# Issuing some of the weight loads in mid-run, in pieces, in a kernel that mixes sliding-window attention and a SwiGLU block

## The chip, the cores and the metric

The kernel runs on one core of one Trainium2 chip. The metric is the device time of one execution in microseconds (us), median of the runs. The engines are TensorE (PE; its weight loads are listed apart as PEld), VectorE (DVE), ScalarE (ACT), GpSimd (POOL) and SyncE (SP), which issues nearly all DMAs. The times of the profile come from one profiled execution.

## The reference

Shapes: S = 2048 tokens, D = 512, 32 heads of 16, window W = 256, F = 1376, all bf16.

```python
x = A_x
g = sigmoid((x * gate_w).sum(-1, keepdims=True))
# A: attention of 32 heads, causal, each query sees the last 256 keys
qkv = (x @ wqkv).reshape(B, S, 3, H, Dh).transpose(2, 0, 3, 1, 4)
scores = einsum("bhqd,bhkd->bhqk", q, k) * (Dh ** -0.5)
mask = (idx[:, None] - idx[None, :] >= 0) & (idx[:, None] - idx[None, :] < W)
p = softmax(where(mask, scores, -1e9))
a = einsum("bhqk,bhkd->bhqd", p, v).transpose(0, 2, 1, 3).reshape(B, S, D) @ wo
# B: SwiGLU
b = einsum("bsf,fd->bsd", silu(x @ w1) * (x @ w3), w2)
out = g * a + (1 - g) * b
```

## The kernel before

All weights stay in SBUF: w1, w3 (512 x 1376), w2 (1376 x 512), the Q, K, V weights (512 x 1536) and the output weights `wo` (512 x 512). x is held transposed in `xT`, in four quarters of 512 tokens. Its first quarter is loaded plain and turned by TensorE; the other three are turned by DMA transposes (`turn_x`, four DMAs of 512 tokens x 128 columns each). w1, w3 and the Q, K, V weights come in column pieces (`load_w`).

`opening` (L301) issues, in this order on SP: half of the first x rows, K weights, Q weights, first pieces of w1 and w3, V weights (first 256 columns of each of K, Q, V), x quarter 1 (counted from 0), w1 columns 256 to 768 and w3 the same, w1 and w3 columns 768 to 1376, x quarter 2, w2 in two DMAs, x quarter 3, `wo`, and the second 256 columns of K, Q, V. The engines' constants are made beside this.

Everything else is given to a planner (`Plan`). Each step has an engine, a duration, the steps it depends on, a due time and buffers that it takes and frees. `emit` lists the steps greedily: it takes the engine that can start earliest, and on it, of the steps that can start then, the one with the earliest due time. The result is a fixed order of instructions on each engine; on the chip the engines wait for each other by semaphores alone, and the planner's times have no force. When a load is in is told to the planner by the table `landed` (L337).

The attention runs over c = 0 to 3, each of 8 heads (128 columns of Q, K, V). For each c: projections of K and Q (L425) and V (L483) for each quarter, scores in blocks of 128 keys (`main_batch` L544, `edge_batch` L594), exponentials on ACT (L548, L598), masks on POOL (L553, L558, L611), the products with V (`pv`, L684), and a normalization on DVE that ends in the tile `OT` (L718). c = 0 and 1 use the first 256 columns of K, Q, V, c = 2 and 3 the second.

The SwiGLU block runs over four quarters of tokens (`tcb`), each over eleven pieces f of F: gate and up products (L809), Tanh on ACT (L819), two products on DVE (L823, L829) into `hT`. The last piece is only 96 wide. 64 of its rows go through `wA`; the other 32 are computed by tokens (`tail_columns`, L769, with `wB`), end on DVE in `hb` (L783), and are turned into `hX` by four DMA transposes on SP (`tr_b`, L793). `wA` and `wB` are copied out of w1 and w3 on POOL (L747). Then the products with w2 follow (L859) and an eviction scaled by 1 - g. The output projection (L889), the sum (L893) and the stores (L899) come last.

Semaphores make SP wait in its own order: a DMA stands behind all that were listed on SP before it.

## Time and profile before

| | |
|---|---|
| median of 3 runs | 238.67 us (238.44 to 240.37) |
| profiled execution, its time | 242.65 us |
| its span, first to last instruction | 240.9 us |
| PE busy | 229.0 us, 95% of the span |
| DVE, ACT, POOL busy | 185.6, 178.4, 154.5 us |
| PE by line, share of the chain that ended last | L809 28%, L859 16%, L425 11%, L684 9%, L544 8% |
| "issue" in that chain | 4% |
| DMA queue q1 (SP's transfers) | 10.59 MB |
| instruction queues q8 and q14 | 0.48 MB in 29 packets, 0.07 MB in 8 |

How to read it: the page divides the span into 40 equal slices of 6.02 us. A digit gives an engine's busy share of a slice in tenths, "PEclk" the clock that TensorE was granted, in tenths of full speed, "DMA" the mean busy share of the core's 16 DMA engines, and "GB/s" what they moved. The chain of waits goes back from the last instruction to what released each step; "issue" is time in which the engine waited for nothing that the profile shows. In a table of groups or waits, `a <-b` names what ended a wait.

SP's issues, in order of time (start, length and count; the length runs from the first issue of the row to the end of its last, waits included):

```profile
4.97 5.11 SPq L288 DMA_TRANSPOSE xT<-in_A_x_dram  x4
10.12 2.56 SPq L295 DMA_DIRECT2D w_sb<-in_B_w_dram  x4
12.73 7.53 SPq L288 DMA_TRANSPOSE xT<-in_A_x_dram  x4
20.30 0.58 SPq L320 DMA_DIRECT2D w_sb<-in_B_w_dram  x1
20.93 0.68 SPq L322 DMA_DIRECT2D w_sb<-in_B_w_dram  x1
21.66 6.00 SPq L288 DMA_TRANSPOSE xT<-in_A_x_dram  x4
27.70 0.58 SPq L324 DMA_DIRECT2D wo_sb<-in_A_wo_dram  x1
28.33 2.66 SPq L295 DMA_DIRECT2D wqkv_sb<-in_A_wqkv_dram  x3
31.10 174.76 SPq L793 DMA_TRANSPOSE hX<-hb  x16
```

### The profile page before, as it was taken

Reading aid. Unit: us, or ns where it says so; the run is one execution under the profiler, and the core shown is the slowest. Engines: PE = TensorE matmul, PEld = TensorE weight load, DVE = VectorE, ACT = ScalarE, POOL = GpSimd, SP = SyncE. Lnnn points to the kernel's source line nnn. Section 1 sums busy time; section 2 is a strip of 40 time slices with the busy share of each in tenths; the row PEclk is TensorE's granted clock in tenths of the full one; section 3 lists DMA queues with packets and bytes.
Section 4 is the critical chain, followed back from the end, with each engine's and each line's share of the span. In section 5 each row is a group of like instructions: output and inputs, shape, how many; then the busy total and the mean of one; then the engine's idle time right before and its main releaser. Section 6 shows DMA issues by size and latency. Waiting matters only on the chain.

```text
span 240.9 us, 8477 instructions
## 1 busy us (share of the span) xinstructions
PE 229.0 (95%) x3700; PEld 119.0 (49%) x3738; DVE 185.6 (77%) x322; ACT 178.4 (74%) x153; POOL 154.5 (64%) x257
## 2 busy tenths in 40 slices
PE   8999679999999999999999999999999999999994
PEld 8554423645553454545555555545454546354542
DVE  5477927697779895986878797798876978987945
ACT  3589818887679898878689898987789898976000
POOL 7169655498776768476577786774859785856000
PEclk9999958999999999999999999999999999999999
DMA  7999990000000001000000001000000001020322
GB/s 200 200 346 234 208 238 6 3 4 0 3 5 0 3 3 22 3 4 3 3 3 3 4 0 25 3 0 5 4 0 3 3 1 23 6 67 24 100 79 87
DMA packets 20413, 11.59 MB, mean 48 GB/s; under 512 B 9656, under 2 KB 20376, under 8 KB 20376
## 3 DMA queue, kind: packets, MB, share of 16 engines
q1 hardware_dynamic: 19680, 10.59, 18.7%
q8 instruction: 29, 0.48, 0.9%
q10 hardware_dynamic: 696, 0.46, 0.6%
q14 instruction: 8, 0.07, 0.1%
HBM read 6.85 MB, written 2.10 MB: 37 GB/s over the span
## 4 chain that ended last, share of the span: by engine, by line
PE 90%; issue 4%; ACT 2%; DVE 2%; DVEq 0%; ACTq 0%
PE ch L809 28%; PE ch L859 16%; PE ch L425 11%; PE ch L684 9%; PE su L544 8%; PE ch L483 6%; PE ch L889 5%; PE su L594 2%; PE su L299 1%; PE ch L769 1%; ACT Ee L598 1%; ACT tt L819 1%; PE ch L362 1%; DVE hT L829 1%; DVE h L823 1%
## 5 line engine op out<-in xcount | busy, mean ns | idle before, releaser
L548 ACT ACTIVATE Em<-su 128x2048 bf16<-128x2048 f32 x60 | 112.6, 1877 | 19.5 <-PE su L544 16.7
L809 PE MATMUL ch<-xT,w_sb 128*128 128x512 bf16 x301 | 79.3, 388 | 1.9 <-issue 1.0
L553 POOL TENSOR_SCALAR_AFFINE_SELECT Em<-Em 64x512 bf16<-64x512 bf16 x60 | 42.5, 709 | 37.0 <-ACT Em L548 32.4
L611 POOL TENSOR_SCALAR_AFFINE_SELECT Ee<-Ee 64x1024 bf16<-64x1024 bf16 x32 | 37.2, 1162 | 16.1 <-ACT Ee L598 14.9
L809 PEld LDWEIGHTS <-w_sb 128*128 128x128 bf16 x320 | 29.1, 99 | 35.9 <-issue 8.8
L823 DVE SCALAR_TENSOR_TENSOR h<-tt,ch 128x512 bf16<-128x512 bf16 (+1 forms) x44 | 29.7, 678 | 14.4 <-ACT tt L819 13.9
L859 PE MATMUL ch<-w_sb,hT 128*128 128x512 bf16 x152 | 38.3, 380 | 0.9 <-issue 0.8
L558 POOL TENSOR_SCALAR_AFFINE_SELECT Em<-Em 64x512 bf16<-64x512 bf16 x56 | 36.8, 658 | 3.3
L501 POOL COPY vs<-vs 64x256 bf16<-64x256 bf16 (+1 forms) x80 | 31.6, 395 | 9.8 <-DVE vs L496 6.6
L598 ACT ACTIVATE Ee<-su 128x2048 bf16<-128x2048 f32 x16 | 30.0, 1877 | 7.3 <-PE su L594 5.4
L425 PE MATMUL ch<-xT,wqkv_sb 128*128 128x512 bf16 (+1 forms) x128 | 33.6, 371 | 0.6 <-issue 0.3
L829 DVE SCALAR_TENSOR_TENSOR hT<-h,ch 128x512 bf16<-128x512 bf16 x40 | 27.1, 677 | 7.6 <-PE ch L809 5.5
L819 ACT ACTIVATE tt<-ch 128x512 bf16<-128x512 f32 (+1 forms) x44 | 26.0, 594 | 6.4 <-DVE vs L496 3.3
L684 PEld LDWEIGHTS <-vs 128*17 128x17 bf16 x1664 | 20.5, 92 | 6.3 <-issue 5.1
L859 PEld LDWEIGHTS <-hT 128*128 128x128 bf16 x160 | 14.3, 98 | 16.9 <-issue 2.5
L684 PE MATMUL ch<-Em,vs 128*17 128x256 bf16 (+2 forms) x672 | 22.5, 242 | 0.0
L684 PE MATMUL ch<-Ee,vs 128*17 128x64 bf16 x992 | 22.1, 193 | 0.0
L483 PEld LDWEIGHTS <-xT 128*128 128x128 bf16 x256 | 15.7, 98 | 8.1 <-issue 4.8
L425 PEld LDWEIGHTS <-wqkv_sb 128*128 128x128 bf16 x136 | 12.5, 99 | 13.7 <-issue 2.7
L544 PE MATMUL su<-qT,kz 32*128 32x256 bf16 x240 | 17.4, 280 | 0.6
L544 PE MATMUL su<-qT,k 32*128 32x256 bf16 x240 | 16.8, 270 | 0.0
L544 PEld LDWEIGHTS <-kz 32*128 32x128 bf16 x240 | 6.0, 91 | 19.2 <-issue 17.4
(77 smaller groups left out, 252.5 us busy)
## 6 DMA issues: line engine op xcount, KB each, us to landing
out_dram<-ot SPq DMA_DIRECT2D x15, 128.0 KB, 1.7
wqkv_sb<-in_A_wqkv_dram SPq DMA_DIRECT2D x5, 256.0 KB, 5.4
w_sb<-in_B_w_dram SPq DMA_DIRECT2D x1, 1280.0 KB, 7.0
w_sb<-in_B_w_dram SPq DMA_DIRECT2D x2, 608.0 KB, 8.5
w_sb<-in_B_w_dram SPq DMA_DIRECT2D x2, 512.0 KB, 4.5
w_sb<-in_B_w_dram SPq DMA_DIRECT2D x2, 256.0 KB, 4.8
wo_sb<-in_A_wo_dram SPq DMA_DIRECT2D x1, 512.0 KB, 5.4
xs<-in_A_x_dram SPq DMA_DIRECT2D x1, 256.0 KB, 2.9
```

Of the source, the lines that this page charges most:

```text
L425: nc.tensor.matmul(pst[:, t0:t1], lhsT=wqkv_sb[:, dc, col + c * P:col + (c + 1) * P], rhs=xT[:, dc, tq * 512 + t0:tq * 512 + t1], start=(d ...
L501: nc.gpsimd.tensor_copy(out=v_of(to, base, a), in_=v_of(half, 0, a))
L544: nc.tensor.matmul(su[:, s, a * 256:(a + 1) * 256], lhsT=head_keys(r, t, a), rhs=qT[r, q0:q0 + 256], start=True, stop=True)
L548: nc.scalar.activation(out=Em[job.at["Em"]][:], in_=su[:].rearrange("p s (a q) -> p s a q", a=2), func=ACT.Exp, scale=SCALE)
L553: nc.gpsimd.affine_select(out=e, in_=e, pattern=[[0, 8], [1, KB]], compare_op=ALU.is_ge, fill=0.0, base=0, channel_multiplier=-1)
L558: nc.gpsimd.affine_select(out=e, in_=e, pattern=[[0, 8], [-1, KB]], compare_op=ALU.is_ge, fill=0.0, base=-1, channel_multiplier=1)
L598: nc.scalar.activation(out=Ee[ej.at["Ee"]][:].rearrange("p s t k q -> p s (t k q)"), in_=su[:], func=ACT.Exp, scale=SCALE)
L611: nc.gpsimd.affine_select(out=e, in_=e, pattern=[[0, 4], [0, 4], [1, KB]], compare_op=ALU.is_ge, fill=0.0, base=0, channel_multiplier=-1)
L684: nc.tensor.matmul(po[32 * s:32 * s + VW, lo - 512 * w:hi - 512 * w], lhsT=vs[:, i, a * VW:(a + 1) * VW], rhs=mov, start=(n == 0), stop=(n ...
L809: nc.tensor.matmul(ch[job.at["ch"]][:], lhsT=wA[:, dc, :] if joint else w[:, dc, f * P:(f + 1) * P], rhs=xT[:, dc, tcb * 512:(tcb + 1) * 512],
L823: nc.vector.scalar_tensor_tensor(out=h1[job.at["h1"]][ru, :], in0=tt[job.at["tt"]][rg, :], scalar=1.0, in1=ch[job.at["ch"]][rg, :], op0=AL ...
L859: nc.tensor.matmul(bps[:], lhsT=ht[:, mm * P:(mm + 1) * P], rhs=w2_sb[0:fs, f, :], start=(f == 0), stop=(f == NFC - 1))
```

## The change

The loads of w2, of `wo` and of the second half of the Q, K, V weights leave the opening. w2 is loaded in four pieces (four, four and two of its eleven blocks of rows, then the last), each listed on SP behind one of the four `hX` transposes of the first quarter. The second half of Q, K, V and then `wo` become steps of the planner on SP that it may not place before its time 86. In the opening, the last pieces of w1 and w3 are now issued between the DMA transposes of x quarter 2. The planner's dates for x quarters 2 and 3 are altered.

```diff
-    def turn_x(tq):
-        for c in range(NDC):
+    def turn_x(tq, c0=0, c1=NDC):
+        for c in range(c0, c1):
...
+    def load_w2(f0, f1):
+        nc.sync.dma_start(out=w2_sb[:, f0:f1, :], in_=B_w2[f0 * P:f1 * P, :].rearrange("(f p) n -> p f n", p=P))
+    def load_w2_end():
+        nc.sync.dma_start(out=w2_sb[0:FL, NFC - 1, :], in_=B_w2[(NFC - 1) * P:F, :])
+    def load_wo():
+        nc.sync.dma_start(out=wo_sb[:], in_=A_wo.rearrange("(c p) n -> p c n", p=P))
...
-        for f0, f1 in ((2 * P, 6 * P), (6 * P, F)):
-            load_w(w1_sb, B_w1, f0, f1)
-            load_w(w3_sb, B_w3, f0, f1)
-        turn_x(2)
-        nc.sync.dma_start(out=w2_sb[:, 0:NFC - 1, :],
-                          in_=B_w2[0:(NFC - 1) * P, :].rearrange("(f p) n -> p f n", p=P))
-        nc.sync.dma_start(out=w2_sb[0:FL, NFC - 1, :], in_=B_w2[(NFC - 1) * P:F, :])
+        load_w(w1_sb, B_w1, 2 * P, 6 * P)
+        load_w(w3_sb, B_w3, 2 * P, 6 * P)
+        turn_x(2, 0, 1)
+        load_w(w1_sb, B_w1, 6 * P, F)
+        turn_x(2, 1, 2)
+        load_w(w3_sb, B_w3, 6 * P, F)
+        turn_x(2, 2, 4)
         turn_x(3)
-        nc.sync.dma_start(out=wo_sb[:], in_=A_wo.rearrange("(c p) n -> p c n", p=P))
-        for b in (1, 0, 2):
-            load_w(wqkv_sb, A_wqkv, b * D + 2 * P, (b + 1) * D)
...
-    landed = {"x": [3.7, 4.45, 12.2, 21.2, 30.2], "w13": [7.1, 8.0, 15.4, 18.7], "w2": 28.0,
-              "qkv": [5.25, 6.15, 8.8, 36.0], "wo": 32.0, "gw": 5.8}
+    landed = {"x": [3.7, 4.45, 12.2, 22.5, 28.5], "w13": [7.1, 8.0, 15.4, 18.7],
+              "qkv": [5.25, 6.15, 8.8], "late": 86.0, "gw": 5.8}
...
-    w2_in, wo_in = arrive(landed["w2"]), arrive(landed["wo"])
+    prev = arrive(landed["late"])
+    for b in (1, 0, 2):
+        prev = add("SP", 0.6, lambda b=b: load_w(wqkv_sb, A_wqkv, b * D + 2 * P, (b + 1) * D), [prev], landed["late"],
+                   lat=0.0 if b < 2 else 4.0)
+    qkv_in.append(prev)
+    wo_in = add("SP", 0.6, load_wo, [prev], landed["late"], lat=4.0)
...
                 res.append(add("SP", 1.25, tr_b, [a] + wx_done.get(tcb - 2, []), due, lat=1.3))
+                if tcb == 0:
+                    load = load_w2_end if mm == 3 else lambda f0=(0, 4, 8)[mm], f1=(4, 8, 10)[mm]: load_w2(f0, f1)
+                    w2_in.append(add("SP", 0.6, load, [res[-1]], due, lat=4.0))
...
-                           hs[f0:f1] + ([prev] if prev else [w2_in]), due,
+                           hs[f0:f1] + ([prev] if prev else w2_in), due,
```

More of the change, by code (lines that the diff above doesn't have):

```diff
@@ L751 @@
     b_ready = {}
+    w2_in = []
     last_up = []
```

## The prediction

> **What bounds the kernel now.** I read the page's slices first, then the chain of waits, the stretches around the one hole that it shows, and the instruction queues in the DMA rows.

> ```profile
> PE   8999679999999999999999999999999999999994
> ...
> PEclk9999958999999999999999999999999999999999
> DMA  7999990000000001000000001000000001020322
> ```

> TensorE is full (digit 9) in nearly every slice. The exceptions are the ends and slices 5 and 6 (24 to 36 us), and only behind them, in slices 6 and 7, is the clock low. The DMA row is full in the first six slices alone. The chain of waits shows what the low digits are:

> ```profile
> 27.78 0.34 PE ch L483 x4
> 28.12 3.41 issue
> 31.53 0.59 PE ch L483 x4
> 32.12 0.43 PE ch L809
> 32.55 0.22 issue
> 32.77 2.77 PE ch L809 x6
> ...
> 39.88 1.73 PE ch L809 x8
> ```

> TensorE stands for 3.41 us and waits for nothing that the profile names. The V product that follows (L483) is the last quarter of one whose other three had run, so its data were there. Afterwards six products of L809 take 2.77 us (0.46 each); later eight take 1.73 (0.216 each). The stretches give the clock:

> ```profile
> 15.34:26.24 10.90, 10.63 (x136) 4.94 (x140) 8.48 (x18) 10.08 (x11) 10.06 (x20) 1.00 1.22 290
> 26.24:28.12 1.88, 1.88 (x112) 1.53 (x101) 1.87 (x7) 1.08 (x4) 1.28 (x2) 1.00 1.34 172
> 28.12:31.53 3.41, 0.00 (x1) 0.00 (x0) 1.43 (x6) 1.62 (x1) 2.36 (x6) 0.86 1.32 131
> 31.53:37.40 5.87, 5.65 (x23) 2.14 (x24) 2.52 (x7) 1.95 (x3) 1.83 (x3) 0.50 0.83 210
> 37.40:48.00 10.60, 10.55 (x190) 5.44 (x191) 7.50 (x14) 8.52 (x11) 5.92 (x11) 1.00 0.01 2
> ```

> Columns: stretch, length, busy time and count of PE, PEld, DVE, ACT, POOL, then clock, DMA share, GB/s. From 31.53 to 37.40 TensorE is busy at clock 0.50, and from 37.40 on busy and at full clock, 10.55 of 10.60 us.

> What it stood for: queue q8 moved 29 instruction pages, 0.48 MB, so 16 KB each; TensorE has 7,438 recorded instructions, 256 to a page. Up to 15.34 it had started 125 + 130 = 255, and a page moves between 15 and 16 us: when one page is used up, another is asked for. Up to 26.24 it has started 255 + 276 = 531, two pages, but the next page moves only in this window, from 28.9 to 29.0 us:

> ```profile
> q1 hardware_dynamic: 89, 0.02, 96.2%
> q8 instruction: 1, 0.02, 69.1%
> ```

> At 28.12 the count is 531 + 213 = 744, close to three pages of 256 (semaphore instructions are not in it). So I read the hole as a code page that came 2.7 us late behind the kernel's own transfers. The page takes 1.1 us (69.1% of 16 engines in 0.1 us), ends at 30.0, and TensorE goes on 1.5 us later. The burst of 160 small instructions at 25.98 to 27.1 (L684) made it need the page so early. This is inferred, not labelled.

> **What the hole costs.** 3.41 us of standing and half of the 5.87 us at half clock, 2.94: 6.35 us. As TensorE is full behind it, all of that reaches the end. The profiled execution took 242.65 us (span 240.9 and 1.75 around it); without the hole it would be 236.3. The median of the runs, 238.67, is 3.98 below the profiled execution and 2.4 above 236.3. I read that as a shorter hole without the slow clock in most runs; the 240.37 among them fits a longer one. So on the median the hole is worth some 2.4 us, not 6.35, and this decides the forecast.

> **The change, part by part.**

> *Taken out of the opening:* six DMAs of SP (w2 1,280 and 96 KB, output weights 512, three of 256). The two of w2 stood ahead of the last four x transposes: 1.41 MB at the 323 GB/s of 22 to 26 us is 4.4 us of transfer.

> *Order on SP.* After the first x transposes end at 10.08 us: loads at 0.64 each (2.56 for four), transposes at 1.88 (7.53 for four). Two w loads end at 11.4, a transpose at 13.3, w1's end at 13.9, a transpose at 15.8, w3's end at 16.5, two transposes at 20.2, the last four (1.28 to 1.88 each) at 25.3 to 27.7, where before they end at 27.66. Their last landed 5.2 us after its issue before and 2.7 in the first group: 26.7 to 31, against 31.5. I take 28, as w2 no longer lies ahead. Third-quarter x: last issue at 18.3 instead of 18.4, landing 3.4 later as before, 22: no change. Nobody waits for x earlier than before, so that saves nothing by itself.

> *w3's last part* is issued at 15.8 instead of 11.9, 3.9 us later. It landed 8.5 us after issue, at 20.4; a load with less ahead took 4.5 to 5.4. So it lands at 20.4 to 24.3. Its first user is the copy on POOL at 22.88 (L747), behind which the masks of line 553 are queued, and behind those the products of L684. Price: 0 to 1.4 us; I take 0 and keep 1.4 (the slot on SP, not the bytes, sets the time).

> *w2 in pieces behind the hX transposes of the first quarter.* The transposes wait for hb (28.10 + 0.25) and were held by SP's loads to 31.10, so they can go at 28.4. Four at 1.41 (5.64) and four loads at 0.64 end at 36.6; the last hX issue moves from about 35.3 to 34.6; the last piece lands 5 to 8.5 us behind its issue, 41 to 45. The first use is L859 at 49.6: 4 us or more of cover. Cost nothing; without the cover, the 4 us at full.

> *Late loads* (three of 256 KB, one of 512): on SP they stand either right behind these (36.6 to 39.2, landed by 46) or behind the second quarter's hX transposes, which in the trace end at 95.3, then 97.9, landed by 104. The first use of these Q, K, V weights is the product at 109.25, of the output weights at 207.4. Cover 5 us even then. No semaphore wait is added that stands long; the product of the first quarter now waits for four loads instead of one.

> *Planner.* Three dates change (21.2 to 22.5, 30.2 to 28.5, w2's gone), so the order on the engines can change from about 20 us on. The trace can't show it. TensorE is full behind 37.4, so an order is worth little except at the ends: I give it 1 us either way, a third of the 3 us between its last product at 237.7 and the span's end.

> *The code page.* At 26.2 us the last x transposes are still in flight, as before, but with 4.4 us less ahead; there is a lull until hX at 28.4. If the page is asked for at 26.2, takes 1.1 us and the same 1.5 to restart, TensorE goes on at 28.85, 0.7 us late; if the 1.5 was itself the crowd, nothing is lost. With the old delay it loses 3.41 again. I take 0.7: a gap this size leaves the clock alone, as all later gaps do.

> The sum, against the profiled execution: 242.65 - 3.41 + 0.7 - 2.94 = 237.0. Against the median, 2.4 - 0.7 = 1.7 off: 237.0 too.

> [...]

> **Rivals.**

> 1. *The hole goes entirely* (0.32): the request meets the lull. For it: from 37.4 to 48, with DMA at 0.01, a page moves and TensorE loses 0.05 us. 236.3, give or take the 1 us of order.
> 2. *The hole isn't the loads' doing* (0.08): it is something that no load order moves. For it: the chain names no releaser. 238.7.
> 3. *w3's end late on POOL* (0.06): 237.0 + 1.4 = 238.4; it decides once it lands after 22.9.
> 4. *Slower: the hole moves and grows* (0.18). Transfers now run without a break from 2 to about 46 us where before they end near 36; the hX transposes lie among w2's pieces, and 256-byte transpose packets were what lay ahead of the late page. If a page is asked for among them and a burst such as L684's (224 instructions, 1.46 us at 45.99) follows, TensorE stands 3.4 us or more, and the clock falls: 6.35 on top of 236.3 is 242.7. It decides at a wait of about 3.4 us, the one that was followed by 0.50. Against it: the page at 35.2, also amid transfers, stopped nothing, since only 47 instructions ran in 5.87 us.

> **Chances and range.** Forecast 0.36, rivals 0.32, 0.08, 0.06, 0.18. One per cent of 238.67 is 2.39 us, about what a measurement of this kernel tells from no change: 236.28 to 241.06. Faster: half of rival 1, whose centre lies on that bound (0.16), and a third of the forecast through the order (0.12): 0.28. Slower: rival 4 and a mishap of order in rival 3 (0.02): 0.20. The rest, 0.52, is within. The range runs from 235.4 (rival 1 less 0.9 of its order) to 241.3, between the forecast and rival 4, which is mostly left out; the forecast's own range is 236 to 238.

> **What would show it.** A gap of TensorE below 1 us around 28, clock 1.00 in slices 5 to 7, x's last quarter landing before 31, and q8's second page moving before 28. SP's late loads either near 37 or near 95, with nobody waiting for them. I am wrong if the profile shows a long gap at another page, if POOL waits before L747, or if the gap at 28 is there with the page on time.

## The result, and the profile after

| | before | changed |
|---|---|---|
| median of 22 runs each | 240.77 us (238.44 to 243.43) | 238.66 us (237.13 to 241.07) |
| profiled execution, its time | 242.65 us | 237.91 us |
| its span | 240.9 us | 236.2 us |
| PE busy | 229.0 us | 225.6 us |

The ratio of the changed kernel to the one before is 0.9923, 95% interval 0.9896 to 0.995: faster by 0.77%, clear of no change, and inside the 1% of the likeliest case. The ratio leaves out the runs that lie more than 1.5% above the fastest of their kernel, so it is not the quotient of the two medians. The level of the kernel before, 238.67 in its first three runs, turned out to be low: the 22 runs have a median 2.1 us higher.

The planner's dates changed, but the compiled lists of instructions of TensorE, VectorE, ScalarE and GpSimd are the same, row by row, in both kernels. Only SP's list differs. So every difference in time comes from when transfers run.

The slices of the page of the changed kernel:

```profile
PE   8999899999999999899999999999999999999994
...
PEclk9999999999999999999999999999999999999999
DMA  7999262000000005200000000000000001010322
```

The low TensorE digits and the low clock in slices 5 to 7 are gone. A slice is 5.9 us here. The DMA row is low in slice 4 (23.6 to 29.5 us), and new work stands in slices 15 and 16 (88.6 to 100.4 us); in slice 16 TensorE has an 8. The chain of waits of the changed kernel (start, length, what), around 28 us and around 96 us:

```profile
27.37 0.34 PE ch L494 x4
27.71 0.76 issue
28.47 0.39 PE ch L494 x4
28.86 0.22 PE ch L824
29.07 0.05 issue
29.13 1.46 PE ch L824 x6
...
95.95 0.34 PE su L605 x30
96.29 0.75 issue
97.04 0.20 PE su L605 x2
```

L494 is the V product that was L483 before. It is cut at the same place, but the gap is 0.76 us instead of 3.41, and six products behind it take 1.46 us instead of 2.77. At 96.29 there is a new gap, inside a batch of scores (L605), with two products of 32 to go. Before, that batch ran through:

```profile
101.79 0.34 PE su L594 x32
102.13 0.75 PE ch L809 x3
```

The late loads stand just ahead of the new gap. SP's issues in the changed kernel:

```profile
84.51 4.92 SPq L805 DMA_TRANSPOSE hX<-hb  x4
89.47 1.68 SPq L295 DMA_DIRECT2D wqkv_sb<-in_A_wqkv_dram  x3
91.19 0.51 SPq L304 DMA_DIRECT2D wo_sb<-in_A_wo_dram  x1
```

An instruction page begins to move behind them; the DMA rows from 94.5 to 94.7 us (queue and kind: packets, MB, share of 16 engines):

```profile
q1 hardware_dynamic: 77, 0.08, 107.6%
q8 instruction: 1, 0.02, 29.2%
```

So the 4.7 us of span divide as follows (times before and after of the same piece of the chain). A row of eleven L859 products starts at 52.99 before and at 47.15 after: 5.84 us won. Nine L809 products start at 99.68 and at 93.85: still 5.83. The V products of 16 start at 102.89 and at 98.00: 4.89. Here 0.94 us is given back, 0.75 of it in the new gap. At the end 4.7 are left.

### The profile page after: what moved, and what is told of

Same layout as the page of the kernel before. It is cut to its first block, busy times and chain, and to the rows that moved or that the text cites. A ratio compares the mean times of both kernels' runs of the same rounds, so it can differ in the third digit from the quotient of the medians.

```text
span 236.2 us, 8479 instructions
## 1 busy us (share of the span) xinstructions
PE 225.6 (96%) x3700; PEld 117.4 (50%) x3738; DVE 185.9 (79%) x322; ACT 178.3 (75%) x153; POOL 154.5 (65%) x257
## 4 chain that ended last, share of the span: by engine, by line
PE 92%; issue 3%; DMA 2%; ACT 1%; DVEq 0%; DVE 0%; ACTq 0%
PE ch L824 30%; PE ch L874 16%; PE ch L436 11%; PE ch L695 9%; PE su L555 8%; PE ch L494 7%; PE ch L904 6%; PE su L605 2%; DMA gwr<-in_gate_w_dram 2%; ACT Ee L609 1%; PE ch L781 1%; ACT L315 0%; DVEq L963 0%; DVE ot L908 0%; ACT tt L834 0%
## 5 line engine op out<-in xcount | busy, mean ns | idle before, releaser
L824 PE MATMUL ch<-xT,w_sb 128*128 128x512 bf16 x301 | 77.2, 380 | 1.9 <-issue 0.8
L622 POOL TENSOR_SCALAR_AFFINE_SELECT Ee<-Ee 64x1024 bf16<-64x1024 bf16 x32 | 37.2, 1162 | 17.0 <-ACT Ee L609 15.8
L824 PEld LDWEIGHTS <-w_sb 128*128 128x128 bf16 x320 | 28.3, 98 | 34.6 <-issue 6.0
L512 POOL COPY vs<-vs 64x256 bf16<-64x256 bf16 (+1 forms) x80 | 31.6, 395 | 7.1 <-DVE vs L507 3.8
L695 PE MATMUL ch<-Em,vs 128*17 128x256 bf16 (+2 forms) x672 | 22.5, 242 | 0.0
L494 PEld LDWEIGHTS <-xT 128*128 128x128 bf16 x256 | 15.6, 98 | 5.4 <-issue 2.1
```

The source lines that it names most:

```text
L494: nc.tensor.matmul(pst[:, mm * w:(mm + 1) * w], lhsT=xT[:, dc, m * P:(m + 1) * P], rhs=rhs, start=(dc == 0), stop=(dc == NDC - 1))
L512: nc.gpsimd.tensor_copy(out=v_of(to, base, a), in_=v_of(half, 0, a))
L622: nc.gpsimd.affine_select(out=e, in_=e, pattern=[[0, 4], [0, 4], [1, KB]], compare_op=ALU.is_ge, fill=0.0, base=0, channel_multiplier=-1)
L695: nc.tensor.matmul(po[32 * s:32 * s + VW, lo - 512 * w:hi - 512 * w], lhsT=vs[:, i, a * VW:(a + 1) * VW], rhs=mov, start=(n == 0), stop=(n ...
L824: nc.tensor.matmul(ch[job.at["ch"]][:], lhsT=wA[:, dc, :] if joint else w[:, dc, f * P:(f + 1) * P], rhs=xT[:, dc, tcb * 512:(tcb + 1) * 512],
```

## The experiments

The theories, both inferred from the traces. **P**: TensorE's instructions come in pages of 256 (q8 moved 29 pages for 7,438 recorded products and weight loads), a page is asked for when an earlier one is used up, and one that comes late behind the kernel's own transfers stops it (the page of the gap before moved from 28.91 to 30.02 us, and TensorE went on at 31.53). The profile shows when a page moves, and no request. **T**: TensorE waits at 28 us for data that the order of the loads delivers late; the last x transpose landed 5.2 us after its issue at 26.4, at 31.6, and TensorE went on at 31.53.

**Shifting the pages, with no load moved.** In the list of instructions the gap before lies at row 702 of TensorE, 66 short of three pages (I put the 66 down to a start that the list doesn't hold), in the changed kernel at rows 702 and 3,004 (190 and 188 modulo 256). These rows count weight loads and products alone. With the other instructions of the list counted too, the weight loads behind the two gaps are rows 709 and 3,013, both 197 modulo 256. So the ends of pages should lie at 190 modulo 256 in the first count. Tiny products in the opening shift all that follows (11 of the 27 large warm-up products become tiny too, which moves no row):

```diff
-        warm_up(WARM)
+        warm_up(16)
+        pad(WARM - 16 + 78)
...
+    def pad(n):
+        for i in range(n):
+            r = 32 * (i % 4)
+            nc.tensor.matmul(su[r:r + VW, 1, 0:KB], lhsT=warm[:, 0:VW], rhs=warm[:, 0:KB],
+                             start=True, stop=True, skip_group_check=True)
```

78 products and their weight loads are 156 rows. The kernel before with this alone:

> Every load as in the kernel before; TensorE only runs 156 more tiny instructions in its opening, so that all later instructions lie 156 places further on in its code pages. Theory P (a code page that comes late): the page that is missing at 28 us is now asked for 156 instructions of work earlier, near 18 us, and is there in time; the gap of 3.41 us at 28 goes though not one load has moved, the clock stays at 1.00 in all slices, the span falls from 240.9 to about 234.6 and the time to about 236.3. Theory T (TensorE waits for a transfer: the last x transpose landed at 31.5, when it went on): the gap stays where it is, 3 us or more, and the span stays near 240.

Measured: 236.12 us (235.81 to 236.49), ratio to the kernel before 0.9817 (0.9769 to 0.9865); span 234.1, clock 1.0. The chain around 28 us:

```profile
26.66 0.34 PE ch L490 x4
27.00 0.34 PE su L601 x32
27.34 0.57 PE ch L490 x8
27.91 0.26 PE ch L816
28.16 0.05 issue
28.21 1.46 PE ch L816 x6
```

The V products (L490) run through. Not one load has moved, so T falls. The pages are still late, as the instruction queue of this kernel between 28.5 and 30 us shows:

```profile
q1 hardware_dynamic: 1053, 0.26, 85.9%
q8 instruction: 1, 0.02, 4.6%
```

By P this page is asked for near 26.0 (row 702); it moves at 29.6, 3.6 us later, about as late as the one that stopped TensorE before (row 446 at 25.50, moved at 28.91: 3.4 us). But its first row, 958, comes only at 35.0, since part of the burst now lies ahead of row 702.

A whole page of shift is the control:

> A control for the shift: the kernel before with 256 tiny instructions more in its opening, a whole page, so every later instruction has its old place within its page. P (code pages): the gap comes back at the same V product near 28 us, 2 to 3.4 us long, and the time is that of the kernel before, 239 to 241. If the padding itself had helped (or shifted something else), the gap stays away and the time is near 236.

Here `pad` has 128 products beyond WARM, with 4 full ones left. Measured: 241.22 us (240.1 to 241.81), ratio 1.0017 (0.9994 to 1.0041). The chain:

```profile
27.82 0.34 PE ch L490 x4
28.15 2.42 issue
30.57 0.59 PE ch L490 x4
31.16 3.17 PE ch L816 x8
```

The gap is back in its old place, at row 958 = 702 + 256, and with it the slow clock (0.50 from 31 to 33 us, eight products in 3.17 us). Padding by itself is worth nothing; where the pages end is worth 4.4 us (240.54 to 236.12, in runs side by side).

The changed kernel shifted:

> The changed kernel with the same 156 tiny instructions. P: its two gaps, 0.76 us at 27.7 and 0.75 at 96.3, both go (pages no longer change inside the bursts there); span 236.2 less about 1.5, near 234.7; time about 236.3. T: the gap at 27.7 stays, as nothing that is loaded has moved; time as the changed kernel, 238.7.

Measured: 236.06 us (236.01 to 236.11), ratio to the kernel before 0.9814 (0.9768 to 0.986), span 234.4; both gaps are gone.

A shift to another place (92 instructions: 46 in place of 78) should make new gaps:

> The changed kernel with 92 tiny instructions instead of 156. With a page needed 256 instructions after it was asked for, and 3.1 us from the one to the other (0.75 to the start of its transfer, 1.0 to 1.1 of transfer, 1.35 until TensorE goes on), the trace of the changed kernel gives new gaps where the transfer queue is empty: about 0.9 us at 41 and 0.5 at 194, and none at 27.7. T: no gap at 41 or 194, the one at 27.7 as before.

Measured in a single run: 236.41 us, span 234.7, nothing at 27.7. Around 41 us:

```profile
40.70 0.32 PE su L562 x6
41.03 0.07 issue
41.10 0.28 PE su L562 x2
```

A cut is there, at rows 1,212 to 1,214 (702 + 512), where the shift puts a page's end. Its size is missed: the weight loads around it start 0.44 us apart and the chain counts 0.07, not 0.9; and at 194 there is none. The 0.75 us that I had put between a row and the start of a page's transfer is not fixed: in the changed kernel's trace one page begins to move at 41.28, 0.71 us after row 958, and the next at 45.23, 0.35 us ahead of row 1,214.

**The late loads.** One date changed: `"late": 86.0` becomes `40.0`.

> The changed kernel, with the four late loads issued right behind w2's pieces (near 36 us) instead of behind the second quarter's hX transposes (89 us). Rival 4 in its small form says the gap of 0.75 us at 96.3 and what else is lost between 87 and 98 (1.1 us against the kernel before) comes from these loads delaying a code page (asked for at 92.2, moved at 94.6): it goes, and no gap takes its place near 40, as the next page there is needed 10 us after the last; span near 235.1, time 1.1 us below the changed kernel. If the loss at 96 is not the loads', it stays.

Measured: 237.46 us (237.13 to 238.29), ratio to the kernel before 0.9879 (0.9819 to 0.9939), span 235.8. The gap at 96 is gone, and the one at 28 is 0.65. The loads now stand at 36.6 to 38.7 and stop nothing. The 1.2 us below the changed kernel's median (not side by side) is as forecast; the span fell by 0.4 only. Its chain says why: a piece of w1 or w3 landed just before the products of L824 that read it, which started at 17.33 in the changed kernel:

```profile
11.36 6.53 DMA w_sb<-in_B_w_dram
17.89 0.05 issue
17.93 0.60 PE ch L824 x2
```

**One part of the change at a time.** Each starts from the kernel before, with the changed kernel's dates for x, which move no row. Only the main lines of each edit are shown. First w2 alone:

```diff
-        nc.sync.dma_start(out=w2_sb[:, 0:NFC - 1, :],
-                          in_=B_w2[0:(NFC - 1) * P, :].rearrange("(f p) n -> p f n", p=P))
-        nc.sync.dma_start(out=w2_sb[0:FL, NFC - 1, :], in_=B_w2[(NFC - 1) * P:F, :])
...
+                if tcb == 0:
+                    load = load_w2_end if mm == 3 else lambda f0=(0, 4, 8)[mm], f1=(4, 8, 10)[mm]: load_w2(f0, f1)
+                    w2_in.append(add("SP", 0.6, load, [res[-1]], due, lat=4.0))
```

> One part of the change alone: w2 goes behind the hX transposes in four pieces; wo and the second Q, K, V pieces stay in the opening, w1 and w3 are not woven in. P: the page asked for at 25.5 has no w2 ahead of it and the x transposes are nearly through, so it moves near 26 to 27; gap 0.7 to 1.5 us, clock 1.00, no gap at 96 (nothing is loaded there); time 1 to 1.5 us below the changed kernel, near 237.4. If the gap is 3 us here too, w2 was not what delayed the page.

Measured: 237.81 us (237.8 to 238.68), ratio 0.9884 (0.9857 to 0.991). The gap is 1.19 us and the clock stays at full behind it (1.00 from 28 to 38 us):

```profile
27.78 0.34 PE ch L490 x4
28.12 1.19 issue
29.31 0.39 PE ch L490 x4
```

Then the late loads alone:

```diff
-        nc.sync.dma_start(out=wo_sb[:], in_=A_wo.rearrange("(c p) n -> p c n", p=P))
-        for b in (1, 0, 2):
-            load_w(wqkv_sb, A_wqkv, b * D + 2 * P, (b + 1) * D)
...
+    prev = arrive(landed["late"])
+    for b in (1, 0, 2):
+        prev = add("SP", 0.6, lambda b=b: load_w(wqkv_sb, A_wqkv, b * D + 2 * P, (b + 1) * D), [prev], landed["late"],
+                   lat=0.0 if b < 2 else 4.0)
+    qkv_in.append(prev)
+    wo_in = add("SP", 0.6, load_wo, [prev], landed["late"], lat=4.0)
```

> Another part alone: the second Q, K, V pieces and wo go behind the second quarter's hX transposes; w2 stays in the opening ahead of x's last quarter. P: what lies ahead of the page at 25.5 is as in the kernel before, so the gap at 28 stays at 2 to 3.4 us, and the 0.75 us at 96 comes on top: time as before or a little above, 240 to 242. If these loads were what delayed the page at 28, the gap shrinks below 1 us.

Measured: 242.17 us (240.46 to 243.77), ratio 1.0075 (1.0034 to 1.0116): slower, at the upper end of what was expected. The gap at 28 is 2.62 us, and the one at row 3,004 is there, larger than in the changed kernel:

```profile
99.50 0.34 PE su L605 x30
99.83 1.31 issue
101.15 0.20 PE su L605 x2
```

Last the weaving of w1's and w3's ends:

```diff
-        for f0, f1 in ((2 * P, 6 * P), (6 * P, F)):
-            load_w(w1_sb, B_w1, f0, f1)
-            load_w(w3_sb, B_w3, f0, f1)
-        turn_x(2)
+        load_w(w1_sb, B_w1, 2 * P, 6 * P)
+        load_w(w3_sb, B_w3, 2 * P, 6 * P)
+        turn_x(2, 0, 1)
+        load_w(w1_sb, B_w1, 6 * P, F)
+        turn_x(2, 1, 2)
+        load_w(w3_sb, B_w3, 6 * P, F)
+        turn_x(2, 2, 4)
```

> The third part alone: w1's and w3's ends among the x transposes of quarter 2, all other loads in the opening as before. P: same bytes ahead of the page at 25.5: gap 2 to 3.4 us, time 239 to 242, the same as before within its interval; no gap at 96.

Measured: 238.78 us (238.71 to 242.69), ratio 0.9913 (0.9881 to 0.9945). The gap is 2.41 us with the slow clock behind it (0.50 from 30 to 33 us), as expected, but the time is 0.9% lower and not the same. What this part wins was not found: the gap is 1 us shorter than in the profile of before, and no shorter than in the control with the whole page of shift, which has the time of before. One lead is the granted clock of the single runs: in three of the five runs here its mean was 1.00 (238.71 to 238.78 us), against 0.999 or 1.00 in 5 of the 19 runs of the kernel before beside them (238.5 to 239.75 us) and 0.992 or 0.993 in the other 14. With so few runs it is not shown that the weaving brought this about.

**A faster version.** Two kernels with the shift of 156 rows and 8 full warm-up products, one with all loads of the change and the late date of 40, one with the loads of the kernel before:

> Changed kernel, late loads right behind w2, 156 instructions of shift, and 8 of the large warm-up products left instead of 16 so that the padding ends before x is in (in the first shifted kernels it ended at 4.2 us and x's transposes on TensorE began 0.29 us later than in the kernel before). P: no gap and full clock; 236.1 less up to 0.3. If the order of the loads matters beyond the code pages, this is below the next kernel by more than the interval.

> The loads of the kernel before with the same shift and the same 8 products. P: as the one above, 235.8 to 236.1, equal within the interval: with the pages out of the way, the order of the loads that the change brings is worth nothing.

Measured: 236.14 us (235.83 to 236.58) and 236.11 (235.53 to 236.63); ratios to the kernel before 0.9859 (0.9824 to 0.9893) and 0.9853 (0.9814 to 0.9892). They are equal: with the ends of pages out of the way, the order of the loads is worth nothing. The shorter warm-up brought nothing over the first shifted kernels (236.12 and 236.06). TensorE's turning of x began at 3.65 us instead of 4.21, but the 16 products took 1.90 us instead of 1.72, and the spans of the profiled executions, the slowest of their six runs, were 0.5 and 0.8 longer. In the one with the loads of the kernel before, a piece of w1 or w3 that landed at 17.97 us held TensorE up; in the other the cause was not found.

## Why the prediction was right and wrong

**What failed.** 237.0 us were forecast and 238.66 measured. The mechanism was right, and two terms of the sum were mis-sized. The hole was worth 4.4 us on the median where 2.4 were put on it, and the late loads, put at nothing, cost 0.94 us of the profiled execution. The forecast time of the changed kernel, 236.3 + 0.7 = 237.0, hangs on the second of these alone.

**The hole is a late code page: right**, and shown by the shift and its control. The counts (255, 531, 744) led to the right cause, but they don't place the ends of pages. They count products that run across the edge of a stretch in both stretches: up to 28.12 us TensorE had started 699, not 744. By P the page that came late was asked for 256 rows ahead of the gap, near row 446, at 25.5 us, and not at 26.2.

**The gap that stays: right, its size in part by luck.** 0.7 us was forecast, 0.76 measured. The forecast had the page asked for at 26.2 us and moved at once, in 1.1 us; in the changed kernel row 446 came near 25.1, and the page began to move 0.75 later and took 1.27. The two errors largely cancel. x's last quarter was issued until 24.5 and landed at 26.1; I had taken 28. The lull was there (no other packet starts between 25.85 and 27.12), the page moved at 25.85, and even so it came late: from row 446 to TensorE's going on at 28.47 it took 3.4 us, and the burst had reached the gap at 27.71, after 2.6. That speaks against rival 1: alone in the queues the page was still too late, so with the pages where they are no order of the loads can be expected to close the gap.

**The clock: right for the profiled execution.** 6.35 us were put on the hole, 2.94 of them the clock. The shifted kernel of before has neither, and its profiled execution took 235.86 us; 236.3 was forecast for a kernel without the hole.

**The hole on the median: wrong.** The step "a shorter hole without the slow clock in most runs", worth 2.4 us, rested on three runs. Over the 7 runs beside it, the kernel before has a median of 240.54, and the shift takes it to 236.12: 4.4 us. The control shows what such a run holds: a gap of 2.42 us with a half clock behind it. So "a wait of about 3.4 us" is also not where the clock begins to fall. The granted clocks of the kernel before, recorded for 36 runs beside the experiments (one of 788.84 us left out), say how often: in 21 the mean clock was 0.992 or 0.993, as in the control's profile (median 240.8 us), and in 15 it was 0.999 or 1.00 (median 239.4). So most runs had the slow clock. The profiled execution, at 0.986 and with 6.83 us of half clock, was a long case.

**The late loads "cost nothing": wrong.** I checked who reads these weights, and there the cover was as worked out: issued behind the second quarter's transposes, used 13 us later (the first at 104.5). What I left out is the reader of the queue that isn't in the program: a code page. By P row 2,750 asks for it; that row came at 92.3 us and the page moved at 94.6, 2.3 us later, with SP's transfers at 86.9% of the 16 engines from 92 to 94.6. In the kernel before, the page moved 0.75 us after the same row (98.16 to 98.91). Rival 4 had the mechanism, and even the burst of 224 instructions, but looked for it among w2's pieces at 28 to 46 us and priced it at 6.35; it came at 96, worth 0.94. There was no such gap among w2's pieces: row 702 came at 28.5, the next page moved from 29.62 to 30.63, and row 958 came only at 40.57.

**So the sum:** 242.65 - 3.41 + 0.76 - 2.94 + 0.94 is 238.0, and the profiled execution took 237.91. Forecast were 237.0; the missing term is the late loads'. The median of the changed kernel, 238.66, lies 0.75 above its profiled execution; what the other runs lose there was not looked into. On the runs, the change is -0.77% where I had -0.7% (1.67 of 238.67): two errors, a hole too small and a gap not seen, that cancel.

**w3 on POOL: right.** The copies that wait for it (L758) start at 22.50, at their place, with no wait. **The planner's order: wrong in a harmless way.** I allowed 1 us either way; not one row moved on any engine but SP. **Rival 2** (not the loads' doing) falls: w2 alone takes the gap to 1.19.

**Where the gain went.** Without the gaps both kernels take 236.1. The kernel before loses 4.4 us to one page, the changed one 2.6 (238.66 - 236.06, not side by side) to two; w2's part wins 1.2%, the late loads by themselves cost 0.75%.

## What to carry to other kernels

Where an engine that is always busy stands for a microsecond or more and the profile names no releaser, look when its instruction queue moved, and count its instructions from one such gap to the next: a packet that ends just before the engine goes on (here 1.35 to 1.51 us in four gaps), and gaps a multiple of the page's count apart (here row 3,004 is 2 short of nine pages behind 702), point to a code page (the first gap itself need not lie at such a multiple: here 702). Moving all instructions by part of a page, with a whole page as the control, tests it. Here moving the page's end out of a burst of small instructions (78 tiny products and their weight loads, 1.8%) cured it more surely than moving transfers (0.77%). And a transfer that is moved to a quiet stretch must be checked against this reader too, not only against those that use its data (here 0.94 us).

## What the runs showed of the hardware

```profile
28.00:30.00 2.00, 0.15 (x3) 0.03 (x1) 1.57 (x6) 1.77 (x1) 1.28 (x3) 1.00 1.58 88
30.00:32.00 2.00, 1.43 (x7) 0.83 (x7) 0.00 (x0) 0.17 (x1) 1.82 (x4) 0.63 1.15 315
32.00:34.00 2.00, 2.00 (x7) 0.59 (x4) 1.09 (x2) 0.00 (x0) 1.15 (x1) 0.51 1.19 300
34.00:36.00 2.00, 2.00 (x17) 0.82 (x16) 1.55 (x7) 1.58 (x2) 0.29 (x1) 1.00 0.87 172
```

- The scatter of the runs was the page's too: 238.4 to 243.4 us in 22 runs before, 235.5 to 236.6 in the 20 runs of the four kernels with the shift of 156 rows.
